# Chosen rows of a mixture-of-depths layer moved through the output by indirect DMA

## The chip, the cores and the metric

One core of one Trainium2 chip runs the kernel. The metric is the device time of one execution in microseconds. A separate execution was taken with the hardware profiler; its trace gives the rows below, with times in microseconds from the start of its span. PE is TensorE (PEld its weight loads), DVE is VectorE, ACT is ScalarE, POOL is GpSimd and SP is SyncE, which issues DMAs.

## What is computed

An RWKV-6 attention over batch 4, 8 heads, 768 tokens and head size 48, and on its output a mixture-of-depths layer: the 128 tokens of each batch with the highest score go through an MLP, and the rest pass unchanged.

```python
for t in range(S):                                   # attention, state is (D, D) per head
    cur = outer(u * k[t], v[t])
    y[t] = r[t] @ (state + cur)
    state = w[t][:, None] * state + outer(k[t], v[t])
x = y.transpose(0, 2, 1, 3).reshape(B, S, H * D)     # (4, 768, 384)
scores = x @ w_gate
out = x.copy()
for b in range(B):
    top = argpartition(-scores[b], 128)[:128]
    ye = relu(x[b, top] @ w1) @ w2                   # 384 -> 1024 -> 384
    out[b, top] = x[b, top] + sigmoid(scores[b, top])[:, None] * ye
```

## The kernel before

The 768 tokens of a batch are cut into six chunks of 128 tokens, one token a partition, so there are 24 chunks in all. A chunk passes through small steps: decays by two scans on VectorE (`decays`, L191 and L203), scaled and transposed keys and receptances (`scaled`), the u term on GpSimd (`own`: rk at L231 and L232, vo at L236), the 128 by 128 score matrices (`scores`), the output y (`outputs`) and the state for the next chunk (`carry`; its product is on GpSimd at L307, its copies on ScalarE at L313). `outputs` adds the u term into x (L280) and takes the score of each token in one VectorE operation (L282). All x of all batches stays in SBUF, in `x_all`.

The mixture of a batch (`mixture`) is a generator. The main loop (L471 to L487) takes up to five of its pieces, each ended by a `yield`, between the attention steps of each chunk of the next batch; the mixture of the last batch has no next batch and runs by itself (L488). Its pieces are, in order:

- the sigmoid of all 768 scores, then all scores of the batch broadcast to every partition by six transposes in two halves (`every`);
- for each chunk, a 0/1 row for every one of its tokens against all 768 tokens (`beats`, with `tie` for equal scores inside the chunk);
- ranks by matmuls of ones with `beats` (L382), and from them `spread`, which holds a one where token t has rank p (L386);
- `spread` transposed (L399) and copied to `pick`; the 128 chosen rows gathered by matmuls of `x_all` with `pick` (L408);
- the MLP: 24 matmuls of 128 columns (L421) and 8 of 384 (L430), all fp32;
- the results sent back to their rows by six matmuls with `spread` (L439), multiplied by the gate and added into `x_all` on VectorE (L443);
- one store of the whole batch, 1152 KB, on SP's queue (L448).

An fp32 matmul that is not a transpose stands in the trace as two instructions. Synchronisation is made by the tile framework. It also fixes, when the kernel is built, the order of the instructions on each engine, from the order in the program and from its own idea of when operands are ready; at run time every engine and every DMA queue works through its list in that order. The pool `psA` has three PSUM buffers, which y, the state product and all tiles of the mixture share. Loads of w, k, r and v run on SP three chunks ahead, with four buffers each and five for v. At the end the kernel reads a flag from the guard sums (`wide`, L536) and branches over a slow general path (`general`), which these inputs don't take.

Of the kernel before, what the change touches and what calls it, by code (L numbers as in the profile page):

```python
# [9 lines left out]
FP32 = mybir.dt.float32  # L10
BF16 = mybir.dt.bfloat16
INT32 = mybir.dt.int32
AF = mybir.ActivationFunctionType
ALU = mybir.AluOpType
AX = mybir.AxisListType

L = 128
DP = 64
# [17 lines left out]
def kernel(  # L36
# [28 lines left out]

    nc = tc.nc
    PSUM = bass.MemoryType.PSUM

    B, H, S, D = r.shape
    C = H * D  # L70
# [11 lines left out]
    assert D <= DP and W <= 512 and C <= 512 and 0 < CAP < S  # L82
# [64 lines left out]
    slot = consts.tile([L, 1], FP32)  # L147
    nc.vector.tensor_copy(out=slot, in_=col[:, 0:1])
    before_f = consts.tile([L, L], FP32)
    nc.vector.tensor_tensor(out=before_f, in0=col, in1=row, op=ALU.is_lt)  # L150

# [16 lines left out]
    x_all = consts.tile([L, B, NCH, C], FP32)  # L168
# [93 lines left out]
    def outputs(t):  # L262
# [16 lines left out]
        x = x_all[:, b, ci, :]  # L279
# [5 lines left out]
        )  # L285
        yield
# [29 lines left out]

    def mixture(b):

        own = score[:, b, :]
        neg = mod.tile([L, NCH], FP32, name="neg", bufs=2)  # L320
        nc.vector.scalar_tensor_tensor(
            out=neg, in0=own, scalar=-1.0, in1=own, op0=ALU.mult, op1=ALU.min
        )
        nc.scalar.activation(out=neg, in_=neg, func=AF.Exp)
        den = mod.tile([L, NCH], FP32, name="den", bufs=2)
        nc.vector.tensor_scalar_add(out=den, in0=neg, scalar1=1.0)
        nc.vector.reciprocal(out=den, in_=den)
        gate = mod.tile([L, NCH], FP32, name="gate", bufs=2)
        nc.vector.scalar_tensor_tensor(
            out=gate, in0=own, scalar=0.0, in1=neg, op0=ALU.is_ge, op1=ALU.max  # L330
        )
        nc.vector.tensor_mul(gate, gate, den)

# [16 lines left out]
        beats = mod.tile([L, NCH, S], BF16, name="beats")  # L350
        for c in range(NCH):
            lo, hi = c * L, (c + 1) * L
            own = score[:, b, c:c + 1]
            if c > 0:
                nc.vector.tensor_scalar(
                    out=beats[:, c, 0:lo], in0=every[:, 0:lo], scalar1=own, scalar2=None,
                    op0=ALU.is_lt,
                )
            tie = mod.tile([L, L], FP32, name="tie", bufs=2)
            nc.vector.scalar_tensor_tensor(  # L360
                out=tie, in0=every[:, lo:hi], scalar=own, in1=before_f,
                op0=ALU.is_equal, op1=ALU.mult,
            )
            nc.vector.scalar_tensor_tensor(
                out=beats[:, c, lo:hi], in0=every[:, lo:hi], scalar=own, in1=tie,
                op0=ALU.is_lt, op1=ALU.add,
            )
            if c < NCH - 1:
                nc.vector.tensor_scalar(
                    out=beats[:, c, hi:S], in0=every[:, hi:S], scalar1=own, scalar2=None,  # L370
                    op0=ALU.is_le,
                )
            yield

        groups = [(c0, min(L, CAP - c0)) for c0 in range(0, CAP, L)]
        gb = 2 if len(groups) == 1 else 1
        spread = mod.tile([L, len(groups), S], FP32, name="spread", bufs=gb)
        for hf in range(2):
            half = slice(hf * NHF * L, (hf + 1) * NHF * L)
            ps = psA.tile([L, NHF * L], FP32, tag="a", name="ps_r")  # L380
            for c in range(NCH):
                nc.tensor.matmul(  # L382
                    ps, ones, beats[:, c, half], start=(c == 0), stop=(c == NCH - 1)
                )
            for gi, (c0, n) in enumerate(groups):
                nc.vector.tensor_scalar(  # L386
                    out=spread[:, gi, half], in0=ps,
                    scalar1=float(-c0), scalar2=slot, op0=ALU.add, op1=ALU.is_equal,
                )
            yield  # L390

        ye = mod.tile([L, len(groups), C], FP32, name="ye", bufs=gb)
        for gi, (c0, n) in enumerate(groups):
            pick = mod.tile([L, NCH, L], FP32, name="pick")
            for hf in range(2):
                ps = psA.tile([L, NHF, L], FP32, tag="a", name="ps_p")
                for q in range(NHF):
                    c = hf * NHF + q
                    nc.tensor.transpose(  # L399
                        ps[:, q, :], spread[:, gi, c * L:(c + 1) * L], ident  # L400
                    )
                nc.scalar.copy(out=pick[:, hf * NHF:(hf + 1) * NHF, :], in_=ps)
                yield

            ps = psA.tile([L, NDC, L], FP32, tag="a", name="ps_x")
            for dc in range(NDC):
                for c in range(NCH):
                    nc.tensor.matmul(  # L408
                        ps[:, dc, :], x_all[:, b, c, dc * L:(dc + 1) * L], pick[:, c, :],
                        start=(c == 0), stop=(c == NCH - 1),  # L410
                    )
            xeT = mod.tile([L, NDC, L], FP32, name="xeT", bufs=2)
            nc.scalar.copy(out=xeT, in_=ps)
            yield
# [18 lines left out]
            nc.scalar.copy(out=ye[:, gi, :], in_=ps)  # L433
            yield

        for c in range(NCH):
            ps = psA.tile([L, C], FP32, tag="a", name="ps_o")
            for gi, (c0, n) in enumerate(groups):
                nc.tensor.matmul(  # L439
                    ps, spread[0:n, gi, c * L:(c + 1) * L], ye[0:n, gi, :],  # L440
                    start=(gi == 0), stop=(gi == len(groups) - 1),
                )
            nc.vector.scalar_tensor_tensor(  # L443
                out=x_all[:, b, c, :], in0=ps, scalar=gate[:, c:c + 1], in1=x_all[:, b, c, :],
                op0=ALU.mult, op1=ALU.add,
            )
            yield
        nc.sync.dma_start(out=out[b].rearrange("(c p) d -> p c d", p=L), in_=x_all[:, b])  # L448
# [42 lines left out]
    def general(gen):  # L491
        u_t = gen.tile([D, H], FP32, name="u_t")
        nc.sync.dma_start(out=u_t, in_=u.rearrange("h d -> d h"))
        for b in range(B):
# [27 lines left out]
            nc.sync.dma_start(out=x_all[:, b], in_=out[b].rearrange("(c p) d -> p c d", p=L))  # L522
            for c in range(NCH):
                scr = lev.tile([L, C], FP32, tag="scr", name="scr")
                nc.vector.tensor_tensor_reduce(
                    out=scr, in0=x_all[:, b, c], in1=wg_bc, scale=1.0, scalar=0.0,
# [41 lines left out]
```

## Time and profile before

| what | value |
|---|---|
| median of 3 runs | 348.49 us (346.61 to 349.78) |
| the profiled execution | 346.81 us, its span 345.0 us |
| TensorE busy | 287.2 us, 83% of the span |
| VectorE busy | 224.5 us, 65% |
| GpSimd busy | 98.2 us, 28% |
| ScalarE busy | 91.5 us, 27% |
| granted TensorE clock, mean | 0.879 |
| HBM traffic | 79 GB/s over the span |

Busy time of an engine is the time in which at least one of its instructions runs; neighbouring matmuls overlap in the trace. The granted clock is a share of full speed. The profiled execution's time stands beside its span because the time holds a little that lies around the span. The chain of waits follows the work that ended last back to the start, each step to what released it.

### The profile page before, as it was taken

The numbers are of one execution on the slowest core, as the hardware profiler recorded it, in microseconds if no ns is written. First come the engines' busy times: TensorE is split into PE (matmuls) and PEld (weight loads), VectorE is DVE, ScalarE is ACT, GpSimd is POOL, SyncE is SP. The second block draws the span as 40 slices with busy tenths as digits, with TensorE's granted clock in tenths as the row PEclk, the third lists the DMA queues.
The fourth block names the chain that finished last, engine by engine and source line by source line (L and its number), as shares of the span: only waits on it lengthen the run. The fifth ranks groups of instructions, "written<-read, shape, count | busy, mean of one in ns | idle before, by whom it ended". The sixth has DMA issues, their size and how long they took to land.

```text
span 345.0 us, 5575 instructions
## 1 busy us (share of the span) xinstructions
PE 287.2 (83%) x2178; PEld 241.7 (70%) x2178; DVE 224.5 (65%) x452; ACT 91.5 (27%) x221; POOL 98.2 (28%) x96
## 2 busy tenths in 40 slices
PE   0149797989888999969998999978998999969980
PEld 0038796978776977858877967867886977847840
DVE  6148778678998527959898526859888416873040
ACT  1143233352444121323254121323313111211100
POOL 1154555363033614424400805414400200200000
PEclk9999769596999999985599999966579999996997
DMA  7999946254662014584351105664100000300004
GB/s 255 251 199 175 150 84 101 47 111 74 116 100 39 3 23 91 146 132 91 67 116 24 20 7 92 173 104 91 25 0 2 0 2 0 119 21 2 0 0 146
DMA packets 104737, 27.56 MB, mean 80 GB/s; under 512 B 99968, under 2 KB 104320, under 8 KB 104704
## 3 DMA queue, kind: packets, MB, share of 16 engines
q1 hardware_dynamic: 103264, 23.99, 38.8%
q10 hardware_dynamic: 1440, 3.15, 2.6%
q8 instruction: 19, 0.31, 0.4%
q14 instruction: 14, 0.11, 0.1%
HBM read 22.41 MB, written 4.72 MB: 79 GB/s over the span
## 4 chain that ended last, share of the span: by engine, by line
PE 49%; DVE 24%; issue 10%; POOL 6%; SPq 4%; ACT 2%; DMA 1%; POOLq 0%; DVEq 0%; ACTq 0%
PE ps_y L275 11%; PE ps_t L180 8%; PE ps_h L421 5%; PE ps_y L269 5%; PE ps_f L430 5%; PE ps_s L245 5%; DVE left L203 4%; DVE right L191 4%; PE ps_x L408 4%; PE ps_o L439 3%; PE ps_kv L298 2%; POOL rk L231 2%; DVE sc L251 2%; DVE scr L282 2%; POOL vo L236 2%
## 5 line engine op out<-in xcount | busy, mean ns | idle before, releaser
L275 PE MATMUL ps_y<-v,sc 128*128 128x48 f32 x384 | 64.7, 295 | 9.0 <-DVE sc L251 9.0
L275 PEld LDWEIGHTS ps_y<-v,sc 128*128 128x128 f32 x384 | 60.0, 222 | 11.2 <-DVE sc L251 10.7
L236 POOL TENSOR_TENSOR vo<-v,own 128x384 f32<-128x384 f32 x24 | 24.4, 1018 | 113.3 <-DVE x_all L280 65.7
L269 PE MATMUL ps_y<-s_buf,R 128*128 128x96 f32 x160 | 37.3, 318 | 6.5 <-ACT s_buf L313 6.5
L191 DVE TENSOR_TENSOR_SCAN right<-wz_buf,from_right 128x516 f32<-128x516 f32 x24 | 35.3, 1470 | 6.4 <-ACT wz_buf L188 6.1
L245 PE MATMUL ps_s<-R,K 48*128 48x128 f32 x384 | 38.9, 340 | 0.0
L280 DVE TENSOR_TENSOR x_all<-ps_y,vo 128x384 f32<-128x384 f32 x24 | 13.3, 556 | 36.5 <-PE ps_y L275 34.7
L231 POOL TENSOR_TENSOR rk<-r_buf,k_buf 128x384 f32<-128x384 f32 x24 | 31.9, 1330 | 17.7 <-DMA r_buf<-in_r_dram 17.7
L180 PE MATMUL ps_t<-ident,w_buf 128*128 128x128 f32 x96 | 20.6, 342 | 19.3 <-DMA w_buf<-in_w_dram 16.2
L245 PEld LDWEIGHTS ps_s<-R,K 48*128 48x128 f32 x384 | 31.8, 233 | 6.4 <-issue 3.8
L251 DVE TENSOR_TENSOR sc<-ps_s,before_f 128x512 f32<-128x512 f32 x48 | 30.7, 674 | 6.9 <-PE ps_s L245 6.9
L269 PEld LDWEIGHTS ps_y<-s_buf,R 128*128 128x128 f32 x160 | 27.4, 214 | 8.6 <-ACT s_buf L313 8.5
L203 DVE TENSOR_TENSOR_SCAN left<-wz_buf,from_left 128x516 f32<-128x516 f32 x24 | 32.6, 1360 | 0.0
L180 PEld LDWEIGHTS ps_t<-ident,w_buf 128*128 128x128 f32 x96 | 15.0, 190 | 23.3 <-issue 17.1
L232 POOL TENSOR_TENSOR rk<-rk,u_bc 128x384 f32<-128x384 f32 x24 | 30.7, 1281 | 2.1 <-DMA u_bc<-in_u_dram 0.5
L307 POOL TENSOR_TENSOR state<-mid,right 128x192 f32<-128x192 f32 x16 | 11.2, 698 | 69.0 <-DVE mid L306 68.9
L188 ACT COPY wz_buf<-ps_t 128x512 f32<-128x512 f32 x24 | 14.1, 586 | 60.4 <-PE ps_t L180 50.7
L234 DVE TENSOR_REDUCE own<-rk 128x8 f32<-128x384 f32 x24 | 12.9, 539 | 21.9 <-POOL rk L232 21.8
L443 DVE SCALAR_TENSOR_TENSOR x_all<-ps_o,gate,x_all 128x384 f32<-128x384 f32 x24 | 14.6, 608 | 19.1 <-PE ps_o L439 19.0
L257 ACT COPY kt<-ps_t 128x512 f32<-128x512 f32 x24 | 14.0, 582 | 43.9 <-PE ps_t L180 43.8
L313 ACT COPY s_buf<-state 64x192 f32<-64x192 f32 x40 | 14.0, 350 | 42.1 <-POOL state L307 40.8
L224 DVE TENSOR_TENSOR K<-ps_t,right 128x512 f32<-128x512 f32 x24 | 16.3, 678 | 12.9 <-PE ps_t L180 12.9
(75 smaller groups left out, 460.6 us busy)
## 6 DMA issues: line engine op xcount, KB each, us to landing
w_buf<-in_w_dram SPq DMA_DIRECT2D x24, 192.0 KB, 3.6
k_buf<-in_k_dram SPq DMA_DIRECT2D x24, 192.0 KB, 3.7
r_buf<-in_r_dram SPq DMA_DIRECT2D x24, 192.0 KB, 4.2
v<-in_v_dram SPq DMA_DIRECT2D x24, 192.0 KB, 2.9
out_dram<-x_all SPq DMA_DIRECT2D x4, 1152.0 KB, 5.2
w<-in_moe_w_dram ACTq DMA_DIRECT2D x2, 1536.0 KB, 9.9
u_bc<-in_u_dram SPq DMA_DIRECT2D x1, 192.0 KB, 4.3
wg_bc<-in_moe_w_gate_dram SPq DMA_DIRECT2D x1, 192.0 KB, 4.0
```

What stands on the lines that cost most here:

```text
L180: nc.tensor.transpose(ps[:, j, :], src(j), ident)
L191: nc.vector.tensor_tensor_scan(out=right[:, WS:0:-1], data0=wz[:, WS:0:-1], data1=from_right, initial=0.0, op0=ALU.mult, op1=ALU.add,)
L203: nc.vector.tensor_tensor_scan(out=left, data0=wz[:, 0:WS], data1=start, initial=0.0, op0=ALU.mult, op1=ALU.add,)
L231: nc.gpsimd.tensor_mul(rk, rb[:, :, 0:D], kb[:, :, 0:D])
L232: nc.gpsimd.tensor_mul(rk, rk, u_bc)
L236: nc.gpsimd.tensor_mul(t["vo"], values[n], o.to_broadcast([L, H, D]))
L245: nc.tensor.matmul(ps[:, par, j, :], t["K"][rows, j, :], t["R"][rows, j, :], start=True, stop=True,)
L251: nc.vector.tensor_mul(t["sc"][:, par], ps[:, par], _heads(before_f, HP))
L269: nc.tensor.matmul(y[:, 2 * j:2 * j + 2, :], t["R"][:, j, :], s_bufs[n % len(s_bufs)][:, j], start=True, stop=False,)
L275: nc.tensor.matmul(y[:, h, :], t["sc"][:, par, j, :], vt[:, h, :], start=(ci == 0), stop=(ci == 0 or par == 1),)
L421: nc.tensor.matmul(ps[:, q, :], w1[:, dc, (f0 + q) * L:(f0 + q + 1) * L], xeT[:, dc, :], start=(dc == 0), stop=(dc == NDC - 1),)
L430: nc.tensor.matmul(ps, hid[:, fc, :], w2[:, fc, :], start=(fc == 0), stop=(fc == NFC - 1))
```

## The change

Chunks no longer stay in SBUF. Each chunk's x is stored to the output at once (SP queue), and the mixture works on the output in HBM:

- the comparisons of a chunk cover only its own and later tokens; the tokens ahead of it follow from the same comparisons, by column sums. Their row sums come with the comparison (`won`), the column sums from 21 matmuls with one column of ones, and `behind_n` completes the rank;
- a one-hot compare of the ranks with the slot numbers (`pick`) and six two-column matmuls give the row number of each of the 128 slots;
- GpSimd fetches these 128 rows by an indirect DMA (`xe`), three transposes turn them for the MLP, and their scores and gates are computed anew from the rows;
- the MLP's matmuls are the same, with more `yield`s among them;
- one multiply-add on the 128 rows, and an indirect DMA puts them back.

`dram_disjoint_views(out, B)` gives one view of the output for each batch, so that dependences are tracked batch by batch.

```diff
+    slots = consts.tile([L, L], FP32)          # column number
+    behind = consts.tile([L, S], FP32)         # first block: before_f, then ones
+    behind_n = consts.tile([L, NCH], FP32)     # tokens behind each token
+    ids = consts.tile([L, B, NCH, 2], BF16)    # row number in two parts
...
-    x_all = consts.tile([L, B, NCH, C], FP32)
+    views = dram_disjoint_views(out, B)
...
-        x = x_all[:, b, ci, :]
+        x = lev.tile([L, C], FP32, tag="x", name="x", bufs=3)
...
+        nc.sync.dma_start(out=views[b][b, ci * L:(ci + 1) * L, :], in_=x)
...
+        ahead = mod.tile([L, NCH, S], BF16, name="ahead")
+        won = mod.tile([L, NCH], FP32, name="won", bufs=2)
         for c in range(NCH):
+            lo = c * L
             nc.vector.scalar_tensor_tensor(
+                out=ahead[:, c, lo:S], in0=every[:, lo:S], scalar=score[:, b, c:c + 1],
+                in1=behind[:, 0:S - lo], op0=ALU.is_le, op1=ALU.mult,
+                accum_out=won[:, c:c + 1],
+            )
+            yield
+        ps = psA.tile([L, NCH], FP32, tag="a", name="ps_r")
+        for c in range(NCH):
+            for e in range(c + 1):
+                nc.tensor.matmul(
+                    ps[:, c:c + 1], ahead[:, e, c * L:(c + 1) * L], ones[:, 0:1],
+                    start=(e == 0), stop=(e == c),
+                )
+        rank = mod.tile([L, NCH], FP32, name="rank", bufs=2)
+        nc.vector.tensor_sub(rank, behind_n, won)
+        nc.vector.tensor_add(rank, ps, rank)
+        yield
+        for gi, (c0, n) in enumerate(groups):
+            pick = mod.tile([L, NCH, L], BF16, name="pick")
...
+            nc.vector.tensor_tensor(
+                out=pick, in0=_heads(slots, NCH), in1=at.to_broadcast([L, NCH, L]),
+                op=ALU.is_equal,
+            )
+            ps = psA.tile([L, 2], FP32, tag="a", name="ps_i")
             for c in range(NCH):
                 nc.tensor.matmul(
+                    ps, pick[:, c, :], ids[:, b, c, :], start=(c == 0), stop=(c == NCH - 1)
+                )
+            idx = mod.tile([L, 1], UINT32, name="idx", bufs=2)
+            nc.vector.tensor_scalar(
+                out=idx, in0=ps[:, 0:1], scalar1=ps[:, 1:2], scalar2=None, op0=ALU.add
+            )
+            rows = views[b][0:b + 1].rearrange("b s c -> (b s) c")
+            where = bass.IndirectOffsetOnAxis(ap=idx[0:n, 0:1], axis=0)
+            xe = mod.tile([L, C], FP32, name="xe", bufs=2)
...
+            nc.gpsimd.indirect_dma_start(
+                out=xe[0:n], out_offset=None, in_=rows, in_offset=where,
+                bounds_check=(b + 1) * S - 1, oob_is_err=False,
+            )
+            yield
             ps = psA.tile([L, NDC, L], FP32, tag="a", name="ps_x")
             for dc in range(NDC):
+                nc.tensor.transpose(ps[:, dc, :], xe[:, dc * L:(dc + 1) * L], ident)
             xeT = mod.tile([L, NDC, L], FP32, name="xeT", bufs=2)
             nc.scalar.copy(out=xeT, in_=ps)
             yield
+            own = mod.tile([L, 1], FP32, name="own", bufs=2)
+            nc.vector.tensor_tensor_reduce(
+                out=scr, in0=xe, in1=wg_bc, scale=1.0, scalar=0.0, op0=ALU.mult, op1=ALU.add,
+                accum_out=own,
+            )
...
+                    if q % 2 == 1:
+                        yield
                 nc.scalar.activation(out=hid[:, f0:f0 + 4, :], in_=ps, func=AF.Relu)
                 yield
...
+                if fc % 2 == 1:
+                    yield
+            ye = mod.tile([L, C], FP32, name="ye", bufs=2)
             nc.vector.scalar_tensor_tensor(
+                out=ye, in0=ps, scalar=gate, in1=xe, op0=ALU.mult, op1=ALU.add
+            )
+            nc.gpsimd.indirect_dma_start(
+                out=rows, out_offset=where, in_=ye[0:n], in_offset=None,
+                bounds_check=(b + 1) * S - 1, oob_is_err=False,
+            )
+            yield
```

## Rows read from the trace of the kernel before

**Rows 1.** Busy by stretch: start:end, length, PE PEld DVE ACT POOL, PEclk, DMA share, GB/s.

```profile
35.00:82.20 47.20, 41.47 (x341) 38.27 (x342) 34.89 (x61) 16.63 (x42) 25.57 (x23) 0.77 0.56 93
82.20:155.00 72.80, 66.16 (x546) 55.23 (x545) 53.24 (x109) 22.73 (x55) 23.11 (x22) 0.95 0.44 82
155.00:232.80 77.80, 71.89 (x545) 61.08 (x545) 55.98 (x106) 22.58 (x55) 25.88 (x22) 0.85 0.39 77
232.80:305.00 72.20, 68.42 (x534) 57.39 (x533) 51.01 (x102) 16.42 (x38) 13.01 (x12) 0.87 0.12 31
112.40:133.50 21.10, 21.10 (x163) 17.81 (x162) 8.82 (x17) 3.44 (x7) 6.89 (x7) 1.00 0.16 29
```

**Rows 2.** Groups of TensorE instructions by line: busy us, mean ns, idle before.

```profile
L275 PE MATMUL ps_y<-v,sc 128*128 128x48 f32 x384 | 64.7, 295 | 9.0 <-DVE sc L251 9.0
...
L439 PE MATMUL ps_o<-ye,spread 128*128 128x384 f32 x48 | 19.9, 512 | 0.6 <-ACT ye L433 0.6
...
L408 PE MATMUL ps_x<-pick,x_all 128*128 128x128 f32 x144 | 18.6, 287 | 0.0
...
L382 PE MATMUL ps_r<-beats,ones 128*128 128x384 bf16 x48 | 12.9, 362 | 2.8 <-DVE beats L369 1.5 <-DVE beats L364 0.7 <-DVE x_all L280 0.5
...
L382 PEld LDWEIGHTS <-ones 128*128 128x128 bf16 x48 | 4.9, 109 | 6.4 <-issue 2.7 <-DVE beats L369 1.7
...
L399 PE MATMUL ps_p<-ident,spread 128*128 128x128 f32 x24 | 4.5, 314 | 0.2 <-DVE spread L386 0.2
...
L534 PE MATMUL ps_w<-ones_f,total 128*1 128x1 f32 x2 | 0.2, 164 | 0.0
```

**Rows 3.** Groups of VectorE instructions by line.

```profile
L443 DVE SCALAR_TENSOR_TENSOR x_all<-ps_o,gate,x_all 128x384 f32<-128x384 f32 x24 | 14.6, 608 | 19.1 <-PE ps_o L439 19.0
...
L360 DVE SCALAR_TENSOR_TENSOR tie<-every,score,before_f 128x128 f32<-128x128 f32 x24 | 10.6, 443 | 1.3 <-ACT every L343 1.2
L355 DVE TENSOR_SCALAR beats<-every,score 128x128 bf16<-128x128 f32 (+4 forms) x20 | 8.7, 436 | 0.0
L364 DVE SCALAR_TENSOR_TENSOR beats<-every,score,tie 128x128 bf16<-128x128 f32 x24 | 8.1, 337 | 0.0
L369 DVE TENSOR_SCALAR beats<-every,score 128x640 bf16<-128x640 f32 (+4 forms) x20 | 8.1, 404 | 0.0
...
L386 DVE TENSOR_SCALAR spread<-ps_r,slot 128x384 f32<-128x384 f32 x8 | 4.8, 599 | 0.0
```

**Rows 4.** POOL's multiply (min/median/max), a wait (total, times, longest), DMA landings.

```profile
L231 POOL TENSOR_TENSOR rk<-r_buf,k_buf x24: 992/1058/1995, 15.1 to 244.3; 128x384 f32<-128x384 f32 x24
...
ACT s_buf L313 <- POOL state L307: 40.8, 14, 4.5
...
v<-in_v_dram SPq DMA_DIRECT2D x24, 192.0 KB, 2.9
...
out_dram<-x_all SPq DMA_DIRECT2D x4, 1152.0 KB, 5.2
```

**Rows 5.** The chain of waits in order of time, 300 to 345: start, length, what.

```profile
305.03 0.56 DVE x_all L280
...
306.74 0.48 ACT every L343
...
319.41 0.49 ACT xeT L413
...
319.94 5.62 PE ps_h L421 x48
325.56 5.18 PE ps_f L430 x16
...
335.47 0.62 DVE x_all L443
```

**Rows 6.** Busy time by stretch in the tail, columns as in Rows 1.

```profile
312.00:314.20 2.20, 1.94 (x8) 1.07 (x7) 1.22 (x3) 0.48 (x1) 0.00 (x0) 0.50 0.00 0
314.20:319.90 5.70, 5.17 (x37) 4.98 (x36) 0.00 (x0) 0.96 (x2) 0.00 (x0) 0.83 0.01 3
```

More of the change, by code (lines that the diff above doesn't have):

```diff
@@ L6 @@
 from concourse import mybir
+from concourse.bass_types import dram_disjoint_views
 from concourse._compat import with_exitstack
@@ L12 @@
 INT32 = mybir.dt.int32
+UINT32 = mybir.dt.uint32
 AF = mybir.ActivationFunctionType
@@ L146 @@
     nc.gpsimd.iota(col, pattern=[[0, L]], base=0, channel_multiplier=1)
-    slot = consts.tile([L, 1], FP32)
-    nc.vector.tensor_copy(out=slot, in_=col[:, 0:1])
+    slots = consts.tile([L, L], FP32)
+    nc.vector.tensor_copy(out=slots, in_=row)
     before_f = consts.tile([L, L], FP32)
     nc.vector.tensor_tensor(out=before_f, in0=col, in1=row, op=ALU.is_lt)
+    behind = consts.tile([L, S], FP32)
+    nc.gpsimd.memset(behind[:, L:S], 1.0)
+    nc.vector.tensor_copy(out=behind[:, 0:L], in_=before_f)
+    count = setup.tile([L, NCH], INT32)
+    nc.gpsimd.iota(count, pattern=[[-L, NCH]], base=S - 1, channel_multiplier=-1)
+    behind_n = consts.tile([L, NCH], FP32)
+    nc.vector.tensor_copy(out=behind_n, in_=count)
+    number = setup.tile([L, B, NCH, 2], INT32)
+    nc.gpsimd.iota(number[:, :, :, 0], pattern=[[S, B], [L, NCH]], base=0, channel_multiplier=0)
+    nc.gpsimd.iota(number[:, :, :, 1], pattern=[[0, B], [0, NCH]], base=0, channel_multiplier=1)
+    ids = consts.tile([L, B, NCH, 2], BF16)
+    nc.vector.tensor_copy(out=ids, in_=number)
     from_right = consts.tile([L, WS], FP32)
@@ L314, in carry @@
         yield
+    groups = [(c0, min(L, CAP - c0)) for c0 in range(0, CAP, L)]
     def mixture(b):
[L319 to L332, printed above, removed]
         every = mod.tile([L, S], FP32, name="every")
@@ L375, in mixture @@
[L375 to L380, printed above, removed]
+            lo = c * L
+            nc.vector.scalar_tensor_tensor(
+                out=ahead[:, c, lo:S], in0=every[:, lo:S], scalar=score[:, b, c:c + 1],
+                in1=behind[:, 0:S - lo], op0=ALU.is_le, op1=ALU.mult,
+                accum_out=won[:, c:c + 1],
+            )
@@ L381, in mixture @@
             for c in range(NCH):
                 nc.tensor.matmul(
-                    ps, ones, beats[:, c, half], start=(c == 0), stop=(c == NCH - 1)
+                    ps, pick[:, c, :], ids[:, b, c, :], start=(c == 0), stop=(c == NCH - 1)
                 )
[L385 to L389, printed above, removed]
@@ L390, in mixture @@
-            yield
[L392 to L403, printed above, removed]
+            idx = mod.tile([L, 1], UINT32, name="idx", bufs=2)
@@ new lines, in mixture @@
+            nc.scalar.activation(out=neg, in_=neg, func=AF.Exp)
+            den = mod.tile([L, 1], FP32, name="den", bufs=2)
+            nc.vector.tensor_scalar_add(out=den, in0=neg, scalar1=1.0)
+            nc.vector.reciprocal(out=den, in_=den)
+            gate = mod.tile([L, 1], FP32, name="gate", bufs=2)
+            nc.vector.scalar_tensor_tensor(
+                out=gate, in0=own, scalar=0.0, in1=neg, op0=ALU.is_ge, op1=ALU.max
+            )
+            nc.vector.tensor_mul(gate, gate, den)
```

56 lines of the change are left out of this document (15 added, 41 removed).

## The prediction

> **What bounds it now.** I read the granted clock and engine busy time by stretch first, then the groups by line, then the chain of waits at the end. The stretches are cut at the starts of the addition that writes a chunk's x (L280). The first of them, 35.0 to 82.2, is five chunk intervals of batch 0, with nothing of the mixture beside them; the next three are six chunks each, with the mixture of the batch before woven in [rows 1]. The reader should see that TensorE is the fullest engine in all four: 41.5 of 47.2 us without the mixture, and 66.2 of 72.8, 71.9 of 77.8 and 68.4 of 72.2 with it, while VectorE has 53.2, 56.0 and 51.0 there. One chunk interval, 112.4 to 133.5, is TensorE alone: 21.1 of 21.1 us, against 8.8 of VectorE.
>
> A busy share hides the clock, so I count full-clock microseconds (length times granted clock). Without the mixture a chunk takes 47.2 / 5 = 9.44 us at 0.77, or 7.3. The three mixed stretches give 72.8 x 0.95 + 77.8 x 0.85 + 72.2 x 0.87 = 198.1, or 66.0 a batch at a mean of 0.89. Six unmixed chunks are 43.6 of these, so one mixture takes 22.4. In time a mixed batch is 74.3 us on average, an unmixed one 56.6, so a mixture costs 17.7 us. This repeats three times; the fourth mixture is bare, in the 40 us from 305.0 to the end.
>
> **Removed from TensorE, per batch.** The four matmul groups that go (selection by one-hot rows, return by one-hot rows, rank sums, transposes of the one-hot rows) have 18.6 + 19.9 + 12.9 + 4.5 = 55.9 us of busy time over four batches, 14.0 each [rows 2]. Groups overlap, since one matmul starts before another has ended: the sixteen matmul groups, from 64.7 down to 0.2, add up to 341 us where the engine's busy time is 287.2, a factor of 0.84 that I apply: 11.8.
>
> **Added to TensorE.** 21 one-column and 6 two-column matmuls on bf16 one-hot or comparison tiles. No such matmul is in the trace. The dearest thing about one is its weight load, 128 columns of bf16: 109 ns by the load of the rank sums [rows 2]. They come to 27 x 0.109 = 2.9 us; the ends are 0, if they fill gaps, and 27 x 0.362 = 9.8, by the whole 384-column rank matmul. I take 2.9, for the load is the same one. Three transposes of the fetched rows: 3 x 0.19 = 0.6 by the removed transposes (4.5 / 24). Net 11.8 - 3.5 = **8.3 us a batch off TensorE**.
>
> **VectorE.** Out go tie, three kinds of beats, spread and the six additions into x: 10.6 + 8.7 + 8.1 + 8.1 + 4.8 + 14.6 = 54.9, or 13.7 a batch [rows 3]. In come six comparisons of 768 down to 128 columns, each with a sum beside it. The same operation takes 0.34 us for 128 columns and 0.61 for 384, so 1.06 ns a column more: 6 x 0.34 + 1920 x 0.00106 = 4.1. No row here prices the sums; I put 0.5 for six, between 0 and a 128-column operation each, 2.0. The one-hot compare over 768 columns is 1.0, the recomputed score and the final multiply-add 0.61 each, three small ones 0.34 each or less: 7.8. Net 5.9 off. I book no time for it, as VectorE is not the fuller engine; it gives a floor instead: 56.6 + 7.8 = 64.4 us a batch, the unmixed pace with all the new VectorE work in line.
>
> **ScalarE** loses two copies of pick and one of ye and stays under a third busy: zero, hidden by TensorE. The new constants (memset, iotas, casts) fall in the first 35 us, where the loads are awaited: zero; were that cover gone, some 2 us once.
>
> **SP's queue.** 24 stores of 192 KB replace four of 1152 KB: the same bytes, earlier. Each waits for x of its chunk, and the loads behind it on SP wait too. Those loads already wait for TensorE to release their buffers, and x is written within about a microsecond of that, so I book zero; the other end is one landing of 2.9 us per chunk.
>
> **POOL's queue.** Two indirect transfers a batch. The trace has none. What a fetch keeps POOL for I put between 0 and POOL's slowest multiply of 1.995, and take that multiply's median, 1.06. It lands between 2.9 (a 192 KB load) and 5.2 (a 1152 KB store) [rows 4]; I take 2.9, the same bytes. In the mixed stretches TensorE has attention work to do meanwhile, so I book zero. Behind a waiting transfer on POOL stand rk, vo and the state update; that is a rival below. POOL's own multiply varies from 0.992 to 1.995 us. [...]
>
> **Mixed batch, summed.** 66.0 - 8.3 = 57.7 full-clock microseconds. At 0.89 that is 64.8 us, at the worst mixed clock, 0.85, 67.9. Thinner TensorE work gives me no reason to expect a better clock, so I take 0.86: 67.1, above the floor of 64.4. Gain 74.3 - 67.1 = 7.2 a batch, **21.5 us** for three.
>
> **The bare tail.** Before, x is written at 305.03, the broadcast scores end at 307.22, the MLP runs from 319.94 to 330.74, x is finished at 336.09, and 8.9 us follow to the end [rows 5]. After, every comparison needs the broadcast of the second half, so they start at 307.2: 4.6 to 311.8; last rank matmul and two small operations 0.8; one-hot 1.0; six matmuls 0.65; index 0.35: 314.6. Fetch 1.06 + 2.9 = 4.0 (ends 2.9 and 7.2): 318.6. Three transposes 0.6, the same copy as before and hand-offs 0.6: 319.8. So the round trip to the output costs what the one-hot selection cost. The MLP is 10.8 at the clock of before, ending at 330.6. But TensorE idles ahead of it now. [...] End 332.6, multiply-add 0.65: 333.3 against 336.09. The six return matmuls go; the scatter's issue and landing (4.0, ends 2.9 and 7.2) fit into the 8.9 that I keep. Gain **2.8**.
>
> [...]
>
> **Sum.** 21.5 + 2.8 = 24.3 off the profiled execution's 346.81: 322.5. That execution lies 0.5% under the median of 348.49; I say 323.
>
> **Rivals.** *The clock falls (slower).* [...] Place: the three mixed stretches. 57.7 / c is the batch. At the unmixed stretch's 0.77 it is 74.9, worse than now; the gain is gone at 0.765, and at 0.72 it is 80.1: 346.8 + 17.5 - 2.8 = 361. For: 0.77 where TensorE is thinnest, and 0.85 in the second mixed stretch although TensorE was 71.9 of 77.8 busy [rows 1]. Against: the thinning lies in the densest part, and the MLP is issued in eight small portions instead of three, so it fills thin stretches. [...] 13 in 100.
>
> *POOL is held.* A fetch stands at the head of POOL for its indices, and the state update behind it is late. ScalarE's copies of the state already wait 40.8 us for it, 4.5 at the longest [rows 4]. Another 4.5 for each of six transfers is 27: 349, no change. For: the queue is in order. Against: POOL is 28% busy, and of its four operations a chunk the state update alone is urgent. 12 in 100, some part of it at half the price, 336.
>
> *Only the packed interval shrinks.* Elsewhere the pace is that of TensorE and VectorE waiting in turn, as in the unmixed stretch, and freed time there is idle. Of what goes, the selection stands right ahead of the MLP in that interval: 18.6 / 4 x 0.84 = 3.9, and 3 x 3.9 + 2.8 = 14.5, so 332. 15 in 100.
>
> **How the numbers follow.** Forecast 60 in 100: 307 to 332. The low end is a clock of 0.92, between the mixed stretches' 0.87 and 0.95: 62.7 a batch, 3 x 11.6 + 4.8 = 39.6 off; the floor gives by 1.7 then, since the unmixed pace it rests on was itself at 0.77. The range ends at 343: a clock of 0.78 (74.0 a batch), or POOL at three quarters of its price; the packed interval alone lies inside. Within 1% (about what a measurement here can tell from no change) and slower share what is left of the clock and POOL: 7 and 9; faster 84.
>
> **What would show it.** Right: mixed batches near 67 us at a granted clock of 0.85 or more, no 21 us interval, MLP of the tail starting some 15 us after the last x, at half clock. Wrong: a clock under 0.77 there; ScalarE waiting for the state well over 41 us; a fetch over 7 us from issue to use.

## The result: faster by 3%, less than half of the forecast gain

| | before | after |
|---|---|---|
| median of 4 runs each, same chip | 349.13 us (346.61 to 351.36) | 338.26 us (337.42 to 340.11) |
| the profiled execution, its span | 346.81 us, 345.0 us | 339.10 us, 337.3 us |
| granted TensorE clock, mean | 0.879 | 0.770 |

The ratio is 0.9698, with a 95% interval of 0.9615 to 0.9781. The forecast was 323 us (307 to 343). The sign was right and the time lies in the range, but 24.3 us were forecast to go and the two profiled executions differ by 7.7. Executions of one kernel differ by some per cent, so ratios and intervals take only those within 1.5% of their kernel's fastest (none is given where that leaves one), and medians and ranges take all.

### The profile page after: what moved, and what is told of

Its sections match the earlier page's. It is cut to its first block, busy times and chain, and to the rows that moved or that the text cites. A ratio compares the mean times of both kernels' runs of the same rounds, so it can differ in the third digit from the quotient of the medians.

```text
span 337.3 us, 5344 instructions
## 1 busy us (share of the span) xinstructions
PE 272.4 (81%) x2034; PEld 239.5 (71%) x2034; DVE 207.9 (62%) x411; ACT 85.5 (25%) x209; POOL 111.6 (33%) x108
## 4 chain that ended last, share of the span: by engine, by line
PE 58%; DVE 17%; DMA 7%; issue 7%; SPq 5%; POOL 3%; ACT 1%; POOLq 0%; DVEq 0%; ACTq 0%
PE ps_y L295 15%; PE ps_h L444 9%; PE ps_t L200 9%; PE ps_y L289 7%; PE ps_s L265 6%; PE ps_f L455 6%; DVE left L223 4%; DVE right L211 4%; PE ps_kv L319 3%; DMA xe<-out_dram,idx 3%; DMA r_buf<-in_r_dram 2%; DVE ahead L361 2%; DVE scr L302 2%; SPq L121 2%; DVE sc L271 1%
## 5 line engine op out<-in xcount | busy, mean ns | idle before, releaser
L295 PE MATMUL ps_y<-v,sc 128*128 128x48 f32 x384 | 71.0, 318 | 7.6 <-DVE sc L271 7.6
L295 PEld LDWEIGHTS ps_y<-v,sc 128*128 128x128 f32 x384 | 67.7, 248 | 9.2 <-DVE sc L271 8.7
L289 PE MATMUL ps_y<-s_buf,R 128*128 128x96 f32 x160 | 42.5, 357 | 10.4 <-ACT s_buf L334 10.4
L300 DVE TENSOR_TENSOR x<-ps_y,vo 128x384 f32<-128x384 f32 x24 | 13.4, 558 | 60.3 <-PE ps_y L295 60.3
L265 PE MATMUL ps_s<-R,K 48*128 48x128 f32 x384 | 42.4, 354 | 0.0
L289 PEld LDWEIGHTS ps_y<-s_buf,R 128*128 128x128 f32 x160 | 32.3, 250 | 11.8 <-ACT s_buf L334 11.8
L211 DVE TENSOR_TENSOR_SCAN right<-wz_buf,from_right 128x516 f32<-128x516 f32 x24 | 36.9, 1536 | 5.9 <-ACT wz_buf L208 5.9
L252 POOL TENSOR_TENSOR rk<-rk,u_bc 128x384 f32<-128x384 f32 x24 | 34.0, 1421 | 1.8 <-DMA u_bc<-in_u_dram 0.5
L444 PE MATMUL ps_h<-xeT,w 128*128 128x128 f32 x192 | 32.5, 346 | 0.6 <-ACT xeT L414 0.6
L444 PEld LDWEIGHTS ps_h<-xeT,w 128*128 128x128 f32 x192 | 31.4, 259 | 1.3 <-ACT xeT L414 1.0
L208 ACT COPY wz_buf<-ps_t 128x512 f32<-128x512 f32 x24 | 14.1, 585 | 59.3 <-PE ps_t L200 58.8
L200 PE MATMUL ps_t<-ident,r_buf 128*128 128x128 f32 x96 | 20.8, 355 | 6.6 <-DVE K L244 6.6
```

What stands on the lines that cost most here:

```text
L200: nc.tensor.transpose(ps[:, j, :], src(j), ident)
L211: nc.vector.tensor_tensor_scan(out=right[:, WS:0:-1], data0=wz[:, WS:0:-1], data1=from_right, initial=0.0, op0=ALU.mult, op1=ALU.add,)
L252: nc.gpsimd.tensor_mul(rk, rk, u_bc)
L265: nc.tensor.matmul(ps[:, par, j, :], t["K"][rows, j, :], t["R"][rows, j, :], start=True, stop=True,)
L289: nc.tensor.matmul(y[:, 2 * j:2 * j + 2, :], t["R"][:, j, :], s_bufs[n % len(s_bufs)][:, j], start=True, stop=False,)
L295: nc.tensor.matmul(y[:, h, :], t["sc"][:, par, j, :], vt[:, h, :], start=(ci == 0), stop=(ci == 0 or par == 1),)
```

## The profile after

First the stretches, cut at the starts of the addition that writes x (now L300), for comparison with [rows 1]. Columns: start:end, length, busy time of PE, PEld, DVE, ACT and POOL with instruction counts, granted clock, DMA share, GB/s. The first is five chunk intervals without the mixture, the next three are six chunks each with it; the last three are neighbouring chunk intervals of the third stretch, which is the second mixed one.

```profile
34.70:82.30 47.60, 41.43 (x340) 38.64 (x341) 35.01 (x60) 15.10 (x38) 24.03 (x21) 0.76 0.62 105
82.30:156.00 73.70, 67.44 (x509) 59.04 (x509) 51.27 (x96) 23.48 (x60) 29.99 (x26) 0.75 0.53 94
156.00:232.00 76.00, 68.42 (x510) 60.26 (x509) 51.31 (x95) 21.33 (x52) 28.23 (x24) 0.75 0.39 84
232.00:303.30 71.30, 65.33 (x499) 56.82 (x497) 43.86 (x88) 13.84 (x31) 15.87 (x14) 0.75 0.14 37
...
179.10:197.80 18.70, 17.24 (x93) 14.67 (x91) 13.00 (x27) 3.87 (x10) 5.55 (x5) 0.50 0.41 84
197.80:210.30 12.50, 12.50 (x104) 12.20 (x105) 4.79 (x12) 2.37 (x5) 5.17 (x6) 0.81 0.13 33
210.30:222.00 11.70, 11.70 (x91) 8.75 (x90) 8.03 (x14) 3.29 (x8) 3.84 (x4) 1.00 0.45 104
```

A mixed batch takes (73.7 + 76.0 + 71.3) / 3 = 73.7 us against 74.3: the mixture beside attention, where 21.5 us were forecast, gained 3 x 0.6 = 1.8. Yet the work did shrink. In full-clock microseconds (length times clock, idle time included) a batch is 221.0 x 0.75 / 3 = 55.3, against 66.0 before and 57.7 forecast. What came back is the clock: 0.75 against a mean of 0.89. The packed interval of 21.1 us at 1.00, which held the selection and the MLP, is gone. The MLP now stands in two intervals that TensorE fills, 12.50 and 11.70 us, and ahead of them stands one of 18.7 us, with the last ranks, the index and the fetch, in which every microsecond ran at 0.50. At the same place of the second mixed stretch, ahead of the MLP's interval, the kernel before had 10.7 us at 1.00:

```profile
178.30:189.00 10.70, 9.35 (x75) 7.42 (x74) 9.21 (x19) 4.04 (x10) 0.51 (x1) 1.00 0.28 55
```

A busy share does not show this: TensorE is busy for 17.24 of the 18.70 us, with longer instructions: the four transposes of w take 435 ns each there, and 287 in the 10.7 us of before.

The clock over the whole span, in tenths for 40 equal slices, before and then after:

```profile
PEclk9999769596999999985599999966579999996997
```

```profile
PEclk9999859587875569995965559996965559995597
```

Before, most slices stand at 9 with a short dip each batch. After, each mixed batch holds a run of 5s and 6s. How one begins is seen in the list of instructions of the kernel after from 166.8 to 172 us (start, length, instruction, in brackets the idle time before it and what ended it), and then in its stretches:

```profile
166.87 0.60 PE L200 MATMUL ps_t<-ident,K 128*128 128x128 f32 x4
...
167.42 1.80 POOL L252 TENSOR_TENSOR rk<-rk,u_bc 128x384 f32<-128x384 f32 x1
...
168.35 1.55 DVE L361 SCALAR_TENSOR_TENSOR ahead<-every,score,behind 128x640 bf16<-128x640 f32 x1
...
169.92 0.32 DVE L330 TENSOR_TENSOR state<-ps_kv,right 128x192 f32<-128x192 f32 x1
...
170.28 0.71 ACT L334 COPY s_buf<-state 64x192 f32<-64x192 f32 x2 [1.67 <-DVE state L330]
...
171.04 0.46 PE L289 MATMUL ps_y<-s_buf,R 128*128 128x96 f32 x2 [3.57 <-ACT s_buf L334]
```

```profile
170.00:172.00 2.00, 0.56 (x7) 0.48 (x7) 2.00 (x5) 1.29 (x3) 0.00 (x0) 0.98 0.06 6
172.00:174.00 2.00, 1.91 (x18) 1.69 (x20) 2.00 (x7) 0.33 (x1) 0.00 (x0) 0.50 0.00 0
174.00:200.00 26.00, 24.54 (x136) 21.88 (x133) 16.56 (x39) 5.54 (x15) 5.55 (x5) 0.50 0.35 76
200.00:206.00 6.00, 6.00 (x56) 5.70 (x55) 1.28 (x4) 1.30 (x3) 4.67 (x6) 0.78 0.17 34
```

On VectorE a comparison of the mixture stands ahead of the state update, the state's copy on ScalarE waits for that, and TensorE for the copy: 3.57 us idle, with nothing of the mixture to do meanwhile but a few narrow matmuls. The clock fell right behind it and came back only after 200 us, though TensorE was busy for 24.54 of the 26 us from 174 on. The cost is seen on matmuls that the change did not touch, the first MLP layer, before (L421) and after (L444). Columns: instruction, count, busy us, mean ns, idle before:

```profile
L421 PE MATMUL ps_h<-xeT,w 128*128 128x128 f32 x192 | 23.3, 279 | 0.6 <-ACT xeT L413 0.6
```

```profile
L444 PE MATMUL ps_h<-xeT,w 128*128 128x128 f32 x192 | 32.5, 346 | 0.6 <-ACT xeT L414 0.6
L361 DVE SCALAR_TENSOR_TENSOR ahead<-every,score,behind 128x768 bf16<-128x768 f32 (+5 forms) x24 | 17.1, 727 | 0.9 <-ACT every L350 0.9
...
L370 PEld LDWEIGHTS <-ahead 128*128 128x128 bf16 x84 | 4.9, 115 | 6.2 <-DVE ahead L361 4.8 <-issue 0.9 <-DVE from_left L218 0.4
L404 POOL DMA_INDIRECT xe<-out_dram,idx x4 | 4.4, 1097 | 28.4 <-DVE idx L396 28.4
...
L412 PE MATMUL ps_x<-ident,xe 128*128 128x128 f32 x12 | 3.6, 435 | 4.5 <-DMA xe<-out_dram,idx 4.5
...
L386 DVE TENSOR_TENSOR pick<-slots,rank 128x768 bf16<-128x768 f32 x4 | 3.8, 939 | 0.0
```

The tail gained the rest, 34.0 us from the last x (303.27) to the end against 40.0. Its chain of waits, in order of time (start, length, what), and its clock in stretches:

```profile
303.27 0.57 DVE x L300
...
311.46 3.14 DMA xe<-out_dram,idx
314.73 0.89 PE ps_x L412 x3
315.64 0.49 ACT xeT L414
316.17 8.45 PE ps_h L444 x48
324.62 5.18 PE ps_f L455 x16
329.82 0.62 DVE ye L461
```

```profile
309.00:314.70 5.70, 0.65 (x13) 0.45 (x11) 1.67 (x7) 0.00 (x0) 1.06 (x1) 0.50 0.13 35
314.70:324.40 9.70, 9.10 (x51) 8.73 (x52) 1.16 (x7) 1.28 (x3) 0.00 (x0) 0.62 0.01 3
324.40:329.80 5.40, 5.40 (x20) 3.00 (x19) 0.00 (x0) 0.60 (x1) 0.00 (x0) 1.00 0.00 0
```

The first layer takes 8.45 us against 5.62 [rows 5], the second the same 5.18: the clock is back at full only for the second. The last x came 1.8 us earlier and the tail is some 6 us shorter, which together is the difference of 7.7.

## The experiments

The main theory, A in the expectations, is that the change thins TensorE's work and the granted clock then falls, which eats the gain. Against it stand the waits that the change brings: the fetch behind the ranks, GpSimd's queue, the new order of the work. Two tools are used. *Thinning* takes TensorE work out of the kernel before. *Fillers* put matmuls in whose result nothing reads. The framework orders each build anew, so an edit can also move other instructions. By the traces the order on TensorE, VectorE, ScalarE and GpSimd, fillers aside, is that of the kernel after in fill_fetch and in warm_tail; what more work gains there is put down to the clock. In all the others it shifts in places too:

```diff
+    def warm(k):
+        ps = psA.tile([L, 512], FP32, tag="a", name="ps_d")
+        for _ in range(k):
+            nc.tensor.matmul(ps, ones, hot, start=True, stop=True)   # hot: ones, bf16 [L, 512]
```

Mixed batches by the windows of each trace (mean length, mean clock, their product), with the time of the profiled execution and of the kernel's fastest, in us:

| kernel | us a batch | clock | full-clock us | profiled | fastest |
|---|---|---|---|---|---|
| before | 74.3 | 0.89 | 66.0 | 346.8 | 343.0 |
| before_thin | 74.5 | 0.81 | 60.0 | 346.6 | 335.6 |
| before_warm4 | 75.8 | 0.92 | 69.7 | 352.7 | 352.2 |
| after | 73.7 | 0.75 | 55.3 | 339.1 | 337.4 |
| coarse | 75.5 | 0.76 | 57.3 | 346.2 | 339.0 |
| late | 76.9 | 0.71 | 54.6 | 350.2 | 339.7 |
| const_idx | 69.5 | 0.79 | 54.6 | 323.6 | 318.0 |
| plain_fetch | 67.8 | 0.82 | 55.8 | 319.8 | 319.8 |
| fill_fetch | 70.2 | 0.81 | 56.9 | 327.0 | 323.3 |
| fill_cmp | 68.6 | 0.86 | 58.8 | 324.0 | 322.8 |
| warm2 | 68.9 | 0.85 | 58.5 | 324.5 | 317.0 |
| warm4 | 68.7 | 0.89 | 61.3 | 323.9 | 319.1 |
| warm2_late | 64.5 | 0.90 | 57.8 | 311.9 | 311.9 |
| warm2_late4 | 64.1 | 0.90 | 57.7 | 310.7 | 308.3 |

The expectations price eight fillers at some 1.8 full-clock us, as an estimate. Measured against the kernel after, a batch grew by 1.6 with 8 fillers (fill_fetch), 3.5 with 12 (fill_cmp), 3.2 with 16 (warm2) and 6.0 with 32 (warm4), idle time included.

### Thinner work alone: before_thin

```diff
-                for c in range(NCH):          # selection: six chunks
+                for c in range(1):            # one
...
+            if c == 0:                        # return: one matmul, read six times
                 ps = psA.tile([L, C], FP32, tag="a", name="ps_o")
```

> The kernel before with less TensorE work and nothing else changed: the selection uses one chunk of six, and the return matmul runs for one chunk and is used for all six (so the chosen rows and the rows they are added to are not the right ones). About 6.8 us of TensorE a batch go, by 30 of 36 selection and 10 of 12 return matmuls. Theory A: the granted clock of the mixed stretches falls to about 0.8 and most of the gain with it, 336 to 346 us, nearly all of what is won in the tail. Theory B: the clock has no part in it, and a batch gains up to 7 us, about 320 to 328 us with the tail.

344.58 us (335.58 to 347.53), ratio 0.9661, 0.9607 to 0.9715. The mixed stretches of the profiled execution, one of 346.64 us:

```profile
83.40:153.70 70.30, 63.31 (x505) 53.95 (x504) 53.35 (x106) 23.60 (x58) 22.46 (x22) 0.86 0.43 85
153.70:231.90 78.20, 70.85 (x507) 59.46 (x505) 55.98 (x106) 22.68 (x55) 24.29 (x22) 0.76 0.37 76
231.90:306.90 75.00, 66.80 (x495) 55.73 (x493) 50.76 (x105) 15.88 (x35) 11.55 (x12) 0.80 0.12 30
```

6.0 full-clock us a batch were taken off, with no fetch and no rank chain, and in this execution a batch became no shorter (74.5) at 0.81. The three executions behind the ratio, 335.58 to 340.58 us, show 0.817 to 0.841 over the span, where the kernel before shows 0.860 to 0.895, and they gain some 12 us. Three batches of 6.0 at the clock of before, with 2.1 in the tail, would have been some 22. So with less work the clock was lower, and about half of the gain was gone. The order of VectorE's instructions shifted too, and what that did is not separated.

### More work on the kernel after: warm2, warm4

```diff
                 accum_out=won[:, c:c + 1],
             )
+            warm(4)                           # warm2: 2
             yield
...
+            warm(8)                           # warm2: 4
             ps = psA.tile([L, NDC, L], FP32, tag="a", name="ps_x")
```

> The changed kernel with filler matmuls that nobody reads (bf16, 512 columns): two behind each of the six comparisons and four behind the index matmuls of each batch, 16 a batch, about 3.5 us of TensorE at full clock. Theory A (the gain was lost to the granted clock: the three mixed stretches of the changed kernel ran at 0.75 and are 55.3 full-clock us each): the clock there rises to about 0.88, a batch takes (55.3 + 3.5) / 0.88 = 66.8 instead of 73.7 us, time about 318 us. Theory B (the pace is set by TensorE, VectorE and GpSimd waiting for each other, and the clock is only its mirror): fillers bring nothing or cost up to 3.5 us a batch, 338 to 352 us.

> As warm2 with twice the fillers: four behind each comparison, eight behind the index matmuls, 32 a batch, about 7 us at full clock. Theory A: clock 0.92 or more in the mixed stretches, a batch (55.3 + 7) / 0.92 = 67.7 us, time about 320 us, so near warm2. Theory B: 345 to 366 us.

warm2: 324.11 us (316.97 to 327.69, no interval). warm4: 323.77 us (319.11 to 323.92), ratio 0.9271, 0.9186 to 0.9357. The mixed stretches of warm4, and its fillers:

```profile
82.90:150.60 67.70, 62.26 (x541) 50.64 (x540) 50.29 (x96) 23.79 (x60) 30.40 (x26) 0.91 0.53 103
150.60:219.60 69.00, 62.34 (x541) 51.64 (x541) 52.12 (x95) 21.17 (x52) 29.73 (x24) 0.92 0.44 93
219.60:288.90 69.30, 64.66 (x531) 54.75 (x531) 44.40 (x87) 13.98 (x31) 17.20 (x14) 0.85 0.14 38
```

```profile
L345 PE MATMUL ps_d<-hot,ones 128*128 128x512 bf16 x128 | 36.1, 419 | 0.0
```

36.1 us of work for nobody made the kernel 14.5 us faster by the medians. The stretches are at 0.85 to 0.92 and 68.7 us a batch, near the 67.1 of the forecast.

### The same fillers on the kernel before, and in the tail alone: before_warm4, warm_tail

The first has warm(4) behind each chunk's `beats` and warm(8) ahead of the selection; the second is the kernel after with warm(2) and warm(8) at the two places in the last batch only.

> The kernel before with the fillers of warm4: four behind each chunk's comparisons and eight ahead of the selection, 32 a batch. Theory A: its mixed stretches are already at 0.89, so fillers have little to give: (66.0 + 7) / 0.97 = 75.3 us a batch against 74.3, so 345 to 352 us, within 1%. Theory C (fillers would speed up any kernel of this kind, and warm2 and warm4 say nothing of the change): 325 to 338 us.

> Fillers in the last, bare mixture alone: two behind each comparison and eight behind the index matmuls. It prices the clock term of the tail. Theory A: the MLP of the tail, 13.65 us in the changed kernel, runs at full clock in about 10.9, and the time is about 2.8 us under the changed kernel's, 335.5; nothing changes before the tail. If the clock is no cause, or the fillers delay the rank: 338 to 341.

before_warm4: 353.28 us (352.18 to 354.81), ratio 1.0245, 1.0177 to 1.0314. Where the clock is high already, fillers cost time, 2.4% where less than 1% was expected, and the clock rose to 0.92, not 0.97. Its first mixed stretch:

```profile
82.90:159.50 76.60, 72.64 (x578) 59.47 (x577) 53.98 (x108) 22.15 (x55) 22.54 (x22) 0.92 0.40 78
...
```

Matmuls that nothing reads are no gain in themselves: the same fillers gained on the kernel after, with its 0.75 (ratio 0.9271), and cost on the kernel before, with its 0.89. warm_tail: 337.94 us (337.77 to 338.13), ratio 0.9798, 0.9742 to 0.9854. In the chain of its tail the first layer is back at the length of before:

```profile
305.03 0.57 DVE x L302
...
317.83 5.62 PE ps_h L455 x48
323.45 5.18 PE ps_f L466 x16
328.66 0.62 DVE ye L472
```

Its tail is 31.0 us against 34.0, of which the MLP gives 13.65 - 10.80 = 2.85. Its mixed stretches stay at 73.7 us and 0.75. The median hardly moved, and the 335.5 us expected did not come: in its profiled execution the last x is written 1.8 us later, and 1.6 of it is there already at the first x (36.36 against 34.72), ahead of any mixture. Why is not known.

### Which place of the fillers counts: fill_cmp, fill_fetch

warm(2) at the six comparisons only, and warm(8) ahead of the three transposes only.

> Fillers behind the six comparisons alone, two each, 12 a batch (2.6 us at full clock). If the comparisons, in which TensorE has only attention to do, are where the clock is lost: nearly the gain of warm2, 324 to 328 us. If the fetch is the place: 333 to 340 us.

> Fillers behind the index matmuls alone, eight a batch (1.8 us at full clock). If TensorE's wait for the fetch is where the clock is lost: nearly the gain of warm2, 324 to 328 us. If the comparisons are the place: 333 to 340 us in the mixed stretches' part, less up to 2.9 us in the tail.

324.32 us, ratio 0.9368 (0.9315 to 0.9421), and 327.33 us, ratio 0.942 (0.931 to 0.953); the kernel after has 0.9698 (0.9615 to 0.9781). The mixed stretches of fill_fetch:

```profile
83.20:153.50 70.30, 65.17 (x518) 55.18 (x517) 51.67 (x96) 23.46 (x60) 29.93 (x26) 0.82 0.55 99
153.50:226.40 72.90, 65.92 (x518) 56.00 (x517) 51.60 (x95) 21.22 (x52) 28.26 (x24) 0.80 0.41 88
226.40:293.90 67.50, 62.34 (x507) 52.25 (x505) 43.96 (x87) 13.83 (x31) 15.86 (x14) 0.81 0.15 39
```

This is the cleanest test of the clock. The instructions stand in the order of the kernel after, 1.6 full-clock us of work a batch were added (56.9 for 55.3), and a batch is 3.5 us shorter at 0.81 for 0.75. In its second mixed stretch the clock costs 14.6 us (0.20 x 72.9), in that of the kernel after 19.0 (0.25 x 76.0). Either place alone gives half to two thirds of what the fastest execution of warm2 (316.97 us) gains, and more of what its median (324.11) gains. So the thin place is the whole stretch of ranks and fetch, not one gap in it.

### Is it the order or the wait? coarse, late, const_idx, plain_fetch

coarse takes out the two added `yield`s in the MLP; late adds two `yield`s behind the fetch, so that attention steps stand between it and its first reader; const_idx keeps both indirect DMAs but gives them fixed indices; plain_fetch reads 128 fixed rows on SP's queue and keeps the indirect store.

```diff
 # coarse
-                    if q % 2 == 1:
-                        yield
...
-                if fc % 2 == 1:
-                    yield
 # late, behind the fetch
             yield
+            yield
+            yield
 # const_idx
-            where = bass.IndirectOffsetOnAxis(ap=idx[0:n, 0:1], axis=0)
+            where = bass.IndirectOffsetOnAxis(ap=fixed[0:n, b:b + 1], axis=0)
 # plain_fetch
-            nc.gpsimd.indirect_dma_start(...)
+            nc.sync.dma_start(out=xe[0:n], in_=views[b][b, 0:n, :])
```

> The changed kernel without the yields that the change put inside the two MLP layers, so the MLP is issued in three portions again. If theory A holds and the finer portions are what thins TensorE's work: clock in the mixed stretches back to about 0.85, time about 328 us. If theory A holds and what thins it is the work that went (selection, return, ranks), or if theory B holds: within 1% of the changed kernel, 335 to 342 us.

> The changed kernel with two more pieces of attention between the issue of the fetch and the transposes of the fetched rows, and no fillers. Theory A (TensorE is too thinly used to keep the clock; the fetch matters only once the clock is up): clock in the mixed stretches stays near 0.75, 333 to 341 us. Theory D (TensorE standing idle for the rank chain and the fetch, which the order puts ahead of attention, is what lowers the clock): clock up to 0.85 or more, 318 to 325 us.

> The changed kernel with both indirect DMAs kept on POOL's queue but given constant indices (the first 128 rows of the batch, so not the chosen ones); ranks and indices are still computed and read by nobody. If the wait for the rank chain ahead of the MLP is what plain_fetch took away: mixed clock about 0.82 and 325 to 330 us as there. If the indirect DMA itself (POOL's queue, its landing) costs it: near the changed kernel, 335 to 341 us at 0.75.

> The changed kernel with the fetch replaced by a plain load of the first 128 rows of the batch on SP's queue (so the rows are not the chosen ones); ranks, indices and the indirect store remain. The MLP no longer waits for the rank chain, nor POOL for the indices. Theory A: at the same thin work the clock stays under 0.8, 332 to 340 us. Theory D: TensorE no longer waits, clock 0.85 or more, 315 to 325 us, and the tail loses its 9 us of ranks and fetch ahead of the MLP in either case, which alone would give 329.

coarse: 345.29 us, ratio 0.9822 (0.9758 to 0.9887). The finer portions of the MLP are no cause of the loss, since the kernel is no faster without them; by the ratios they may be worth some 4 us of the gain, but the intervals overlap. late: 342.54 us (339.68 to 350.2), ratio 0.9803 (0.9735 to 0.9872). With attention work put behind the fetch the kernel is no faster. Its row in the table is of an execution of 350.2 us; the four behind the ratio show 0.756 to 0.785 over the span, about as the kernel after (0.770 to 0.789). The profile after says why so little was to be had there: of TensorE's 4.5 us of waiting for fetched rows (L412) one wait of 3.8 is in the tail, which leaves 0.7 for the three mixed batches. The wait for the fetch, taken alone, is not the loss.

const_idx: 320.74 us (318.03 to 323.56), ratio 0.9256 (0.919 to 0.9322). Its first mixed stretch is still at 0.74 (72.4 us), the other two at 0.81; the second:

```profile
...
154.90:225.70 70.80, 63.12 (x509) 55.32 (x508) 50.05 (x95) 21.32 (x52) 28.82 (x24) 0.81 0.42 90
...
```

plain_fetch: 326.97 us, ratio 0.947 (0.9398 to 0.9542), with a clock of 0.82 that lies between what theories A and D expected. The indirect transfers are no burden: with them, but without the wait for the ranks, the kernel is at least as fast as with a plain load. So the wait for the chain of comparisons, ranks and index ahead of the MLP very likely has a part in the loss, on TensorE or on GpSimd, neither of which waits there any longer, though the order shifted too. But its removal shows in the clock (0.79 and 0.82 for 0.75) at the same full-clock work, so these two don't separate the wait from the clock. They do show that the amount of work is not the whole reason for the low clock.

### Clock held and fetch covered: warm2_late, warm2_late4, warm1_late, warm4_b0

warm2 with two and with four added `yield`s behind the fetch; the same with two and half the fillers (warm(1), warm(2)); and warm4 with two warm(2) in each chunk of batch 0, which has no mixture beside it.

> warm2 with two more pieces of attention between the issue of the fetch and the transposes of the fetched rows, so that TensorE has other work while the rows come. If the round trip to the output stands in TensorE's way in the mixed stretches: up to 3 us a batch off, about 316 us. If it is hidden, as the prediction booked: within 1% of warm2, 321 to 327 us.

> warm2_late with four more pieces instead of two between fetch and transposes. If the fetch is hidden by two: the same as warm2_late, 313 to 318. If it still shows: 309 to 313.

> warm2_late with half the fillers: one behind each comparison, two behind the index matmuls. Theory A: too few to hold the clock, between late and warm2_late, some 325 us. Theory D: the fillers cost more than they give once TensorE no longer waits, 311 to 316 us.

> warm4 and two more filler groups of two in each chunk of batch 0, the unmixed stretch, which ran at 0.77 and 9.44 us a chunk. Theory A: 7.3 + 0.9 full-clock us at about 0.95 give 8.6 us a chunk, some 4 us off in five chunks, about 320 us where warm4 has 323.8. Theory B (there the pace is TensorE and VectorE waiting in turn): no gain, 323 to 327 us.

warm2_late: 315.62 us (311.9 to 318.99), ratio 0.9078 (0.8982 to 0.9175). warm2_late4: 310.44 us (308.33 to 311.41), ratio 0.8922 (0.8835 to 0.9008), the fastest of all:

```profile
83.40:146.20 62.80, 58.23 (x520) 49.13 (x522) 48.41 (x96) 23.11 (x59) 29.15 (x26) 0.94 0.58 109
146.20:211.80 65.60, 61.57 (x523) 52.42 (x525) 50.53 (x95) 21.05 (x52) 27.97 (x24) 0.87 0.46 97
211.80:275.70 63.90, 59.12 (x511) 50.49 (x513) 44.60 (x88) 14.06 (x31) 16.25 (x14) 0.89 0.17 43
```

The fastest execution of warm2 is 316.97 us. With two `yield`s, which did not help late, the two behind the ratio are 311.9 and 314.37; with four, all lie between 308.33 and 311.41. So these `yield`s gain some 3 to 9 us beside fillers and nothing without them. They also move instructions on every engine, so that the gain comes from the cover under the fetch is argued, not shown. warm1_late, 335.71 us with a wide spread (322.68 to 337.52, no interval), had 72.7 us a batch at 0.73 to 0.81 in an execution of 336.56 us, and a clock of 0.831 over the span in that of 322.68: half the fillers kept the clock up in one execution of four. warm4_b0, 328.88 us (319.86 to 330.51, no interval), shortened the unmixed stretch as meant, to 42.5 us at 0.92, but its mixed batches took 70.9 us against warm4's 68.7, and no run says why. It is inconclusive.

## Why the prediction was wrong in its size

**TensorE's work: right, a little small.** 8.3 full-clock us a batch were booked, 10.7 went (66.0 to 55.3, idle included). The narrow matmuls were booked at 2.9 by their weight loads. These take 115 ns against 109, but overlap: 5.6 us of busy time for the 84 of the ranks and 1.4 for the 24 of the index make 1.75 a batch. The transposes took 0.9 for 0.6.

**The clock: the step that failed.** It read "Thinner TensorE work gives me no reason to expect a better clock, so I take 0.86". That asks the question one way only; the same thinning was a reason to expect a worse one. At 0.86 the measured 55.3 would be 64.3 us a batch; at 0.75 they are 73.7, or 28 us over three batches. A clock under 0.77 is what the prediction itself named as a sign of being wrong. That the clock, and not the order, is where time went is shown by fill_fetch, where more work in the same order makes a batch 3.5 us shorter. What lowered it is shown in part: it is lower with less work (before_thin, 0.81 for 0.89), higher with more (the fillers, 0.81 to 0.89 for 0.75), and higher without the wait for the ranks (const_idx and plain_fetch, 0.79 and 0.82 for 0.75); the shares are open. That selection, rank and return matmuls had filled the places where attention waits is argued from this, not shown.

The rival "the clock falls", given 13 in 100, came true. With the work and the tail as booked, 57.7 / 0.75 = 76.9 us a batch and some 352 us in all, slower than before and outside the range. That the time still lies inside it is luck: 2.4 more full-clock us of work went in each batch, 3.2 us at 0.75, and the tail gave 3.2 us more. The rival's argument, 0.77 where TensorE is thinnest [rows 1], was the better reading. "Against: the thinning lies in the densest part" failed: the MLP still fills TensorE (11.70 of 11.70 us at 1.00), but the interval ahead of it, 10.7 us at 1.00 in the second mixed stretch before (178.3 to 189.0), is now the one of 18.7 us at 0.50. The fillers, more matmuls in the thin place, agree with the rival: 0.75 to 0.81 in fill_fetch.

**The tail: 6.0 for 2.8.** Three terms were off. MLP start 12.9 us behind x, not 14.8: the six comparisons with their sums took 3.7 us for 4.6 (305.36 to 309.08), rank and index 2.1 for 2.8 (to 311.18), and the fetch 3.5 with its hand-over for 4.0 (to 314.73). The end behind the last VectorE operation took 6.9 us where 8.9 were kept. No run shows the 2.0 us for the clock, by which the end of 332.6 lies behind 330.6 and by which the 4.8 in the range's low end exceeds 2.8; in its place the MLP took 13.65 us for 10.80, + 2.85, at 0.62 from 314.7 to 324.4 behind 5.7 us at 0.50, and warm_tail took that back in full.

**GpSimd's queue: rightly booked at zero.** Waits of the kernel after (who, for whom: total us, times, longest):

```profile
ACT s_buf L334 <- POOL state L328: 34.7, 13, 4.1
POOL xe L404 <- DVE idx L396: 28.4, 4, 12.4
...
PE ps_x L412 <- DMA xe<-out_dram,idx: 4.5, 3, 3.8
```

ScalarE waits less for the state than the 40.8 us of [rows 4], though a fetch did hold GpSimd for its indices. An issue took 1.10 us, against 1.06 booked. So the rival that POOL is held did not come true by its own sign, a wait well over 41 us. warm4 has 55.9 us of ScalarE's wait and is faster all the same.

**The floor: not shown to be one.** 64.4 us a batch was put as the floor by VectorE and the unmixed pace; the best version reaches 64.1, in its first stretch 62.8, so it goes a little below, and no run shows that VectorE sets that pace. The comparisons with their sums took 17.1 + 1.9 = 19.0 us, 4.8 a batch, for 4.6 booked. SP's stores and the constants, booked at zero, show little: the first x is written at 34.70 against 35.00, and the five intervals after it, with stores but no mixture, take 47.6 us for 47.2.

**Only the packed interval shrinks** was wrong as a rival for its mechanism: the interval of the selection and the MLP did shrink, from 21.1 us to 12.5 and 11.7 for the MLP's two layers with attention around them, but the one ahead of it grew from 10.7 to 18.7, and the batch as a whole gained only 0.6.

**Open:** how the fall of the clock divides between the work that went and the wait for the ranks, since const_idx and plain_fetch hold some 0.8 without fillers; warm4_b0; and whether 310 us is the end, as the amount of filler was not tuned.

## What to carry to other kernels

Work taken off the engine that bounds a kernel is priced in full-clock microseconds and then divided by a clock that must be forecast on its own (here 55.3 by 0.75, where 0.86 was taken): ask what filled TensorE's waits before, and whether the edit removes it. The test is cheap: matmuls that nothing reads, put in the newly thin place; if the kernel gets faster, and the trace shows the other instructions in the old order, as in fill_fetch, the clock was the loss; if it gets slower, as the kernel before did, it was not. An edit that moves work under a wait should be judged again with the clock held: the `yield`s of late gained nothing alone, and 3 to 9 us with fillers.

## What the runs showed that was not expected

- The granted clock stayed at 0.50 from 172 to 200 us of the kernel after, behind one idle time of 3.57 us, with TensorE busy for 24.54 of the last 26 us. Being busy did not bring it back at once.
- The comparison of 640 columns took 1.55 us where it overlapped GpSimd's multiply of 1.80, and 0.88 in the tail, where GpSimd was idle. The one of 768 columns ahead of it took 1.01 us beside a GpSimd instruction of 1.53, and 1.02 in the tail, so the cause is not shown.
- A fetch of 128 scattered rows of 1536 bytes, 192 KB, took 3.14 us from issue to landing, less than the load of 192 KB in [rows 4] plus its issue on GpSimd.
